# Gate units 0 to 7 as pairs on 64-row halves of TensorE in a fused linear-attention and gated-MLP kernel

## The chip, the cores and the metric

The kernel runs on one core of a Trainium2 chip. The metric is the device time of one execution in microseconds (us). TensorE (PE) does the matrix products and has its own stream of weight loads (PEld), VectorE (DVE) and ScalarE (ACT) take results out of PSUM and do the elementwise work, GpSimd (POOL) makes a few constants, SyncE (SP) issues most of the transfers. PSUM has 8 banks.

## The reference

The input `x` is 2048 tokens of 448 features, in bf16. Two branches start from the same layer norm and are multiplied:

```python
xn = _layernorm(x)
# branch s: 16 heads of 28, phi(t) = where(t > 0, t + 1, exp(t)) + 1e-6
q, k, v = split(xn @ wqkv)
kv  = einsum("bhsd,bhse->bhde", phi(k), v)
z   = einsum("bhsd->bhd", phi(k))
num = einsum("bhqd,bhde->bhqe", phi(q), kv)
den = einsum("bhqd,bhd->bhq", phi(q), z)[..., None] + 1e-6
s = (num / den).reshape(B, S, D) @ wo
# branch g: 448 -> 1792 -> 448
h = relu(xn @ w1 + b1) ** 2
g = silu(h @ w2 + b2)
out = x + s * g
```

## The kernel before

The tokens are cut into 16 tiles of 128, and those into 4 groups of 512. The work of TensorE is a sequence of units, written out in strings by hand at the end of the kernel function:

- `H{g}.{f}` (line 773): the hidden layer's 128 features `f` for the 512 tokens of group `g`. Its result is taken out by a relu with bias, on ACT (line 751) or DVE (line 748), and squared two units at a time, on DVE (line 762) or ACT (line 763), into `r2`.
- `K{t}` (line 716) and `Q{g}.{m}` (line 726): the keys of token tile `t`, and 128 columns of the queries of group `g`. `phi` takes each out by an exponential on ACT (line 694) and two operations on DVE (lines 699 and 706).
- `G{t}`, a gate unit: the product of token tile `t` of `r2` with `w_2`, 14 steps over 1792 features, 448 columns wide. DVE takes it out by adding `b2` (line 1069).
- `S{t}` (line 1171): the last product of the attention branch for a token tile.
- `P{t}` and `X{t}`: layer norm of four token tiles on DVE and ACT (lines 483 to 530), and their transpose into `xT` (two DVE operations, line 550, and 16 DMAs of 32 KB). Units of the group that begins with tile `t` read the result.
- `zs` (line 910): sums of phi(k) over the tokens on DVE. `R0 R1`, `Z`, `D` (lines 853, 924, 948) make the denominators, whose reciprocals go through DRAM and come back spread over the partitions (lines 966 to 1014).

The weights of H, K and Q have 448 rows, which is 3.5 times 128. So these units run in pairs on 64-row halves of the array: `pair` (line 654) runs, in one slot, one matmul of unit `a` on rows 0 to 63 and one of unit `c` on rows 64 to 127, in different PSUM banks. In a first phase `a` has the lower rows and `c` the upper ones, in a second phase they change places, and the first matmul of the second phase waits for the last of the first (`op.sync`). `pe_four` (line 685) lets two pairs alternate, first phases and then second phases, so that the work of the other pair lies between. The units G10 to G13 and all S run in such pairs too, through `weave` (line 1316), which steps each pair named by a word `A|B` each time the word comes up. A pair of gate units has 14 slots in a phase and is stepped four times, 7 slots each time.

The units G0 to G9 go through `gg` (line 1088, matmuls on line 1096) in another form: 14 matmuls on all 128 rows, in two parts of 7. In the strings they stand between pairs on 64 rows: G0 to G3 in one block, and G4, G5, G6 and G7 each alone.

The order on PE and SP is the program's order. For ACT, DVE and POOL, and for the PSUM banks, a planner (`Program.one_pass`, line 98) sorts the operations by modelled durations and due times before the kernel is built. Its model charges `SWITCH` for a change between 128-row and 64-row form, and an operation that empties a PSUM bank is due `BANK_LATE` after the start of the last matmul step that writes the bank. Each engine then executes its own list strictly in order, and waits on semaphores.

Of the kernel before, what the change touches and what calls it, by code (L numbers as in the profile page):

```python
# [18 lines left out]

LAT = {"pe": 0.2, "act": 0.07, "dve": 0.07, "pool": 0.08, "sp": 0.07}  # L20
SWITCH = 0.095
BANK_LATE = 6.5
SWAP = 1
PASSES = 1

# [21 lines left out]
class Program:  # L47
# [50 lines left out]
    def one_pass(self):  # L98
        ops = self.ops
        for op in reversed(ops):  # L100
# [3 lines left out]
            for r in op.reads:  # L104
                if isinstance(r, Buf):
                    late = min(late, self.writer[r].ideal + BANK_LATE)
            span = 14.0 if op.group else 4.5 if op.nbytes else op.dur + LAT[op.home]
# [198 lines left out]
def bass_recurrent_scan__linear_attn_block__dense_activation_squared_relu__prompt_kernel(  # L306
    nc, A_x, A_wqkv, A_wo, B_x, B_w1, B_b1, B_w2, B_b2, out
):
    with ExitStack() as es:
# [226 lines left out]
        def dve_transpose(lo):  # L536
            first = lo == 4 * SWAP
            parts = stage[:, :, :, :, :]
            stays = [("stage", 0), ("stage", 1)]
            if not first:  # L540
                parts = gbuf[:, NT - 5 : NT, :].rearrange("p t f -> p (t f)")[:, 0:2048]
                parts = parts.rearrange("p (b c j k) -> p b c j k", b=4, c=4, j=2)
                stays += [("g", i) for i in range(NT - 5, NT)]
            wide = parts.rearrange("p b c j k -> p (b c j k)").bitcast(f32)
            wide = wide.rearrange("p (b c j k) -> p c b j k", b=4, c=4, j=2)
            for j in range(2):
                src = xn[:, lo + 2 * j : lo + 2 * j + 2, :].rearrange("p t f -> p (t f)").bitcast(f32)
                src = src.rearrange("p (c b i) -> p c b i", c=4, b=4)
                add(
                    "dve", lambda e, _, j=j, src=src: e.transpose(wide[:, :, :, j, :], src),  # L550
                    [(n, lo + 2 * j + t) for n in ("xn", "xd") for t in (0, 1)], [stays[j]] + (stays[2:] if j else []), 0.7, label=f"tr{lo + 2 * j}",
                ).lead = 0.8 * (1 - j)
            for a in range(4):
                for b in range(4):
                    src = parts[32 * a : 32 * a + 32, b, :, :, :].rearrange("p c j k -> p (c j) k")
                    dst = by_group(slice(32 * b, 32 * b + 32), lo // 4).rearrange("p (n k) -> p n k", k=256)
                    by_act = lo == 4 and 4 * a + b > 12
                    op = dma(
                        "act" if by_act else "sp", dst[:, :, 64 * a : 64 * a + 64], src, [("xs", lo, a, b)], 32 * 1024,
                        stays, dur=0.65, slow=1.0,  # L560
                    )
                    op.group, op.lead = ("xs", lo), -8.0 if by_act else 0.0
# [65 lines left out]
        def pe_transpose_two(lo):  # L628
            b = Buf("T")

            def f(e, _):
                v = ps(b)[:, :].bitcast(bf)
                for i in range(8):
                    last = e.transpose(
                        v[:, i * P : (i + 1) * P], xn[:, lo + i // 4, (i % 4) * P : (i % 4 + 1) * P], ident[:, :]
                    )
                return last

            ts = (lo, lo + 1)
            add("pe", f, [(w, i) for i in ts for w in ("xn", "xd")] + ["ident"], [b], 8 * 0.065, mode="128", label=f"T{lo}")  # L640

            def ev(e, eng):
                src = ps(b)[:, :].bitcast(bf)
                dst = xT[:, lo : lo + 2, :, :].rearrange("p t c k -> p (t c k)")
                if eng == "dve":
                    return e.tensor_copy(dst, src)
                return e.activation(out=dst, in_=src, func=AF.Copy)

            add("dve", ev, [b], [("xT", i) for i in ts], 0.68, alts=[("act", 1.05)], label=f"eT{lo}")
# [35 lines left out]
        def pe_four(a, b, c, d):  # L685
            one, two = pair(a, c), pair(b, d)
            for p in (one, two, one, two):
                next(p)
            assert next(one, None) is next(two, None) is None
# [398 lines left out]
        def gg(si):  # L1088
            b = Buf("G")
            g = si // 4  # L1090
            for part in range(2):

                def f(e, _, part=part):
                    last = None
                    for fi in range(7 * part, 7 * part + 7):
                        last = e.matmul(  # L1096
                            ps(b)[:, 0:D], r_cols(slice(0, P), fi, si), w_2[:, fi, :], start=(fi == 0),
                            stop=(fi == NF - 1),
                        )
                    return last  # L1100

                add(
                    "pe", f, [("r2", g, fi) for fi in range(7 * part, 7 * part + 7)] + ["w2"] + ([b] if part else []), [b],
                    7 * MM(D), mode="128", label=f"G{si}.{part}",
                )
                if part:
                    g_bias(si, b)
                yield

        def silu(si):  # L1110
            if not silu_set:
                add(
                    "act", lambda e, _: e.preload_act_table_set("silu_and_others"), ["rden", "actw"], ["actw"], 1.3,
                    label="table2",
                )
                silu_set.append(1)
            gs = gbuf[:, si, :]
            add(
                "act", lambda e, _: e.activation(out=gs, in_=gs, func=AF.Silu), [("g", si), "actw"], [("g", si)], 0.577,  # L1119
                label=f"si{si}",  # L1120
            )
# [133 lines left out]
        def prep(lo):  # L1255
            ln(lo, lo + 2)
            ln(lo + 2, lo + 4)
# [15 lines left out]
        def run(text):  # L1273
            stream = []
            for w in text.split():
                assert not stream or w[0] in "KQHS", w
                if w[0] in "KQHS":
                    stream.append(w)
                    if len(stream) == 4:
                        pe_four(*map(unit, stream))  # L1280
                        stream.clear()
                elif w[0] == "G":
                    for _part in gg(int(w[1:])):
                        pass
                elif w[0] == "g":
                    next(sums.setdefault(w, gg(int(w[1:]))))
                elif w[0] == "X":
                    dve_transpose(int(w[1:]))
                elif w[0] == "T":
                    pe_transpose_two(int(w[1:]))  # L1290
                elif w[0] == "P":
                    prep(int(w[1:]))
                elif w[0] == "A":
                    for _part in token_sum(int(w[1:])):
                        pass
                elif w[0] == "a":
                    next(sums.setdefault(w, token_sum(int(w[1:]))))
                elif w[0] == "R":
                    q_rest(int(w[1:]))
                elif w == "zs":  # L1300
                    zsums()
                elif w == "Z":
                    z_cols()
                elif w == "D":
                    den()
                    spread()
                elif w == "V":
                    fold_wv()
                elif w == "M":
                    fold_wo()  # L1310
                elif w[0] == "I":
                    for v in w[1:].split(","):
                        silu(int(v))
            assert not stream

        def weave(text):
            pairs = {}
            for w in text.split():
                if w not in pairs:
                    pairs[w] = pair(*map(unit, w.split("|")))  # L1320
                next(pairs[w])
            assert all(next(p, 0) == 0 for p in pairs.values())

        hs = lambda g, lo, hi: " ".join(f"H{g}.{i + j}" for i in range(lo, hi, 4) for j in (0, 2, 1, 3)[: hi - i])
        gate = lambda a, b, u, v, more="": weave(
            f"G{a}|G{b} G{a}|G{b} {u}|{v} {more} G{a}|G{b} G{a}|G{b} {u}|{v} {more}"
        )
        run(hs(0, 2, 14) + " Q0.0 K2 Q0.1 K3 g0 g1 P8 g0 g1 G2 G3")
        run("X8 P12 " + hs(1, 0, 12) + " H1.12 K4 H1.13 K5 Q0.2 K6 Q1.0 K7 X12 G4 H2.0 Q1.1 H2.1 Q1.2 G5")
        run(hs(2, 2, 14) + " K8 Q2.0 K9 Q2.1 G6 H3.0 K10 H3.1 K11 H3.2 Q2.2 H3.3 Q3.0 G7 H3.4 K12 H3.5 K13")  # L1330
        run("H3.6 K14 H3.7 K15 zs H3.8 Q3.1 H3.9 Q3.2 H3.10 H3.11 H3.12 H3.13")
        run("R0 R1 a0 Z a0 D I0,1,2,3,4,5,6,7 a0 a0 A1 A2 A3 G8 V G9 M")
        a, b = "G10|G11", "G12|G13"
# [37 lines left out]
```

## Time and profile before

| | us |
|---|---|
| median of 3 runs (lowest, highest) | 146.09 (145.98, 146.63) |
| profiled execution | 146.12 |
| its span, first to last instruction | 144.0 |
| PE busy | 140.0 (97%) |
| DVE busy | 103.8 (72%) |
| ACT busy | 77.4 (54%) |
| weight loads | 71.4 (50%) |

Times in the text are microseconds from the start of the span. A line of the chain of work that ended last gives the start, the length, the engine, what is written, the line of the kernel and the number of instructions. A line of the timeline gives the start, the length from the first start to the last end, and the engine's instructions with their shapes. Starts of matmuls are recorded and their ends are modelled, so the distance from one start to the next is the safer number. In the table of windows each engine's busy time is followed by the number of instructions that started there.

### The profile page before, as it was taken

Reading aid. Unit: us, or ns where it says so; the run is one execution under the profiler, and the core shown is the slowest. Engines: PE = TensorE matmul, PEld = TensorE weight load, DVE = VectorE, ACT = ScalarE, POOL = GpSimd, SP = SyncE. Lnnn points to the kernel's source line nnn. Section 1 sums busy time; section 2 is a strip of 40 time slices with the busy share of each in tenths; the row PEclk is TensorE's granted clock in tenths of the full one; section 3 lists DMA queues with packets and bytes.
Section 4 is the critical chain, followed back from the end, with each engine's and each line's share of the span. In section 5 each row is a group of like instructions: output and inputs, shape, how many; then the busy total and the mean of one; then the engine's idle time right before and its main releaser. Section 6 shows DMA issues by size and latency. Waiting matters only on the chain.

```text
span 144.0 us, 3040 instructions
## 1 busy us (share of the span) xinstructions
PE 140.0 (97%) x1198; PEld 71.4 (50%) x1198; DVE 103.8 (72%) x225; ACT 77.4 (54%) x143; POOL 6.4 (4%) x40
## 2 busy tenths in 40 slices
PE   7999999999999999999999999999999999999991
PEld 7964444554444444444444444445547455555471
DVE  2779898699598799859778888971007736865874
ACT  3566977022588709597878378788239430302311
POOL 7900100000000000000000000000000000000000
PEclk9999999999999999999999999999999999999998
DMA  4999983496232100233000000000199400222032
GB/s 106 313 327 311 331 266 62 68 261 168 45 48 42 17 0 5 36 52 48 14 0 0 0 0 5 0 0 22 16 225 192 81 5 29 97 70 96 32 122 69
DMA packets 23499, 12.89 MB, mean 90 GB/s; under 512 B 14274, under 2 KB 22718, under 8 KB 23486
## 3 DMA queue, kind: packets, MB, share of 16 engines
q1 hardware_dynamic: 21758, 11.40, 30.7%
q10 hardware_dynamic: 1728, 1.31, 4.1%
q8 instruction: 9, 0.15, 0.4%
q14 instruction: 4, 0.03, 0.1%
HBM read 9.23 MB, written 1.90 MB: 77 GB/s over the span
## 4 chain that ended last, share of the span: by engine, by line
PE 96%; DVE 2%; issue 0%
PE pb L773 29%; PE pb L1096 19%; PE pb L1079 7%; PE pb L1171 7%; PE pb L874 6%; PE pb L716 6%; PE pb L726 6%; PE pb L1206 4%; PE pb L1136 3%; PE pb L853 1%; DVE gbuf L1160 1%; PE pb L880 1%; PE pb L816 1%; PE pb L788 1%; PE pb L1023 1%; PE pb L948 1%
## 5 line engine op out<-in xcount | busy, mean ns | idle before, releaser
L773 PE MATMUL pb<-xT,w 64*128 64x512 bf16 x378 | 43.6, 376 | 0.0
L751 ACT ACTIVATE r<-pb,b1f 128x512 bf16<-128x512 f32 x39 | 25.3, 686 | 19.0 <-PE pb L773 18.2
L773 PEld LDWEIGHTS pb<-xT,w 64*128 64x128 bf16 x378 | 18.0, 94 | 22.6 <-issue 1.1
L1096 PE MATMUL pb<-w,r 128*128 128x448 bf16 x140 | 27.7, 353 | 0.0
L1096 PEld LDWEIGHTS pb<-w,r 128*128 128x128 bf16 x140 | 13.2, 98 | 13.9 <-issue 1.2
L748 DVE TENSOR_SCALAR r<-pb,b1f 128x512 bf16<-128x512 f32 x17 | 12.4, 745 | 5.4 <-PE pb L773 5.4
L763 ACT ACTIVATE r<-r 128x1024 bf16<-128x1024 bf16 x15 | 15.7, 1062 | 0.4 <-DVE r L748 0.3
L1191 DVE TENSOR_TENSOR gbuf<-pb,gbuf 128x448 bf16<-128x448 f32 x14 | 8.1, 618 | 6.1 <-PE pb L1171 6.1
L1079 PE MATMUL pb<-w,r 64*128 64x448 bf16 x112 | 11.7, 349 | 0.0
L716 PE MATMUL pb<-w_k,xT 64*128 64x448 bf16 x98 | 11.6, 349 | 0.0
L987 DVE TENSOR_TENSOR pqT<-pqT,xT 128x2048 bf16<-128x2048 bf16 x3 | 3.7, 1218 | 10.7 <-DMA xT<-scr 10.7
L1069 DVE TENSOR_TENSOR gbuf<-pb,b2b 128x448 bf16<-128x448 f32 x14 | 8.5, 617 | 3.6 <-PE pb L1096 2.1
L726 PE MATMUL pb<-xT,w_q 64*128 64x512 bf16 x84 | 11.0, 376 | 0.0
L483 DVE BATCH_NORM_STATS2 st<-x_tok 128x6 f32<-128x448 bf16 x16 | 9.3, 611 | 2.4 <-DMA x_tok<-in_A_x_dram 2.4
L1119 ACT ACTIVATE gbuf<-gbuf 128x448 bf16<-128x448 bf16 x14 | 7.0, 570 | 6.8 <-DVE gbuf L1069 5.9
L1171 PE MATMUL pb<-w_k,pqT 64*128 64x448 bf16 x96 | 10.5, 349 | 0.0
L874 PE MATMUL pb<-pk,xn 128*128 128x448 bf16 x48 | 9.6, 353 | 0.0
L706 DVE SCALAR_TENSOR_TENSOR pk<-pb,pk 128x448 bf16<-128x448 f32 x16 | 9.3, 617 | 0.1
L762 DVE TENSOR_TENSOR r<-r 128x1024 bf16<-128x1024 bf16 x13 | 8.4, 685 | 0.2
L694 ACT ACTIVATE pk<-pb 128x448 bf16<-128x448 f32 x16 | 7.8, 545 | 1.3 <-PE pb L803 0.7
L910 DVE TENSOR_TENSOR zacc<-zacc,pk 128x448 f32<-128x448 f32 x13 | 8.0, 619 | 0.2
L1079 PEld LDWEIGHTS pb<-w,r 64*128 64x128 bf16 x112 | 5.4, 94 | 5.3 <-issue 0.4
(98 smaller groups left out, 141.3 us busy)
## 6 DMA issues: line engine op xcount, KB each, us to landing
out_dram<-gbuf SPq DMA_DIRECT2D x15, 112.0 KB, 1.7
w<-in_B_w_dram SPq DMA_DIRECT2D x1, 1568.0 KB, 9.5
x_tok<-in_A_x_dram SPq DMA_DIRECT2D x3, 448.0 KB, 5.7
xT<-gbuf SPq DMA_DIRECT2D x32, 32.0 KB, 2.0
w<-in_B_w_dram SPq DMA_DIRECT2D x2, 384.0 KB, 5.8
xT<-scr SPq DMA_DIRECT2D x6, 112.0 KB
w<-in_B_w_dram SPq DMA_DIRECT2D x1, 576.0 KB, 5.6
xT<-scr ACTq DMA_DIRECT2D x5, 112.0 KB
```

The lines of the kernel that those rows point to most:

```text
L483: add("dve", lambda e, _: e.bn_stats(st6[:, si, :], x_tok[:, si, :]), [("x", si)], [("st", si)], 0.61, label=f"bn{si}").prio = hp(si, 0)
L706: lambda e, _: e.scalar_tensor_tensor(out=slot, in0=ps(buf)[0:rows, 0:n], scalar=1.0 + 1e-6, in1=slot, op0=ALU.add, op1=ALU.max),
L716: return e.matmul(ps(b)[:, 0:D], x_tile(rows, si, c), w_k[rows, c, :], start=start, stop=stop)
L726: return e.matmul(ps(b)[:, 0:512], w_q[rows, c, m * P : (m + 1) * P], x_group(rows, g, c), start=start, stop=stop,)
L748: return e.tensor_scalar(out=slot, in0=ps(b)[:, 0:512], scalar1=b1f[:, fi : fi + 1], scalar2=0.0, op0=ALU.add, op1=ALU.max)
L751: return e.activation(out=slot, in_=ps(b)[:, 0:512], func=AF.Relu, bias=b1f[:, fi : fi + 1])
L763: return e.activation(out=both, in_=both, func=AF.Square)
L773: return e.matmul(ps(b)[:, 0:512], w_1[rows, c, fi * P : (fi + 1) * P], x_group(rows, g, c), start=start, stop=stop,)
L874: last = e.matmul(ps(b)[:, 0:D], xn_cols(si, c * P, (c + 1) * P), pk[:, si, :], start=(si == 0), stop=(si == NT - 1),)
L1079: return e.matmul(ps(b)[:, 0:D], r_cols(rows, fi, si), w_2[rows, fi, :], start=start, stop=stop)
L1096: last = e.matmul(ps(b)[:, 0:D], r_cols(slice(0, P), fi, si), w_2[:, fi, :], start=(fi == 0), stop=(fi == NF - 1),)
L1171: return e.matmul(ps(b)[:, 0:D], w, msb[rows, c, :], start=start, stop=stop)
```

## The change

G0 to G7 leave `gg` and go through `pair` on 64-row halves. G0|G1 alternates with G2|G3. G4|G5 is interleaved with the pairs H2.0|H2.1 and Q1.1|Q1.2, which before made a `pe_four` between G4 and G5. G6|G7 is interleaved with H3.0|H3.1 and K10|K11, which before made a `pe_four` between G6 and G7; the units H3.2, Q2.2, H3.3 and Q3.0 now come behind G7 and not ahead of it. `weave` passes a word without `|` on to `run`, so that P8 keeps a place inside the block of G0 to G3. `BANK_LATE` goes from 6.5 to 8.0, which changes due times of all PSUM operations in the planner. G8 and later units and the end of the kernel are as before.

```diff
-BANK_LATE = 6.5
+BANK_LATE = 8.0
@@ weave
             for w in text.split():
+                if "|" not in w:
+                    run(w)
+                    continue
                 if w not in pairs:
                     pairs[w] = pair(*map(unit, w.split("|")))
                 next(pairs[w])
@@ the order of the units
-        run(hs(0, 2, 14) + " Q0.0 K2 Q0.1 K3 g0 g1 P8 g0 g1 G2 G3")
-        run("X8 P12 " + hs(1, 0, 12) + " H1.12 K4 H1.13 K5 Q0.2 K6 Q1.0 K7 X12 G4 H2.0 Q1.1 H2.1 Q1.2 G5")
-        run(hs(2, 2, 14) + " K8 Q2.0 K9 Q2.1 G6 H3.0 K10 H3.1 K11 H3.2 Q2.2 H3.3 Q3.0 G7 H3.4 K12 H3.5 K13")
+        run(hs(0, 2, 14) + " Q0.0 K2 Q0.1 K3")
+        weave("G0|G1 G0|G1 G2|G3 P8 G2|G3 G0|G1 G0|G1 G2|G3 G2|G3")
+        run("X8 P12 " + hs(1, 0, 12) + " H1.12 K4 H1.13 K5 Q0.2 K6 Q1.0 K7 X12")
+        weave("G4|G5 G4|G5 H2.0|H2.1 G4|G5 H2.0|H2.1 Q1.1|Q1.2 G4|G5 Q1.1|Q1.2")
+        run(hs(2, 2, 14) + " K8 Q2.0 K9 Q2.1")
+        weave("G6|G7 G6|G7 H3.0|H3.1 G6|G7 H3.0|H3.1 K10|K11 G6|G7 K10|K11")
+        run("H3.2 Q2.2 H3.3 Q3.0 H3.4 K12 H3.5 K13")
         run("H3.6 K14 H3.7 K15 zs H3.8 Q3.1 H3.9 Q3.2 H3.10 H3.11 H3.12 H3.13")
```

`hs(g, lo, hi)` lists the units H of group `g` from `lo` to `hi` in the order in which `pe_four` pairs neighbours.

## The prediction

> **What bounds the kernel now.** I read the first page, then the chain that ended last, then the waits of PE, then the timeline around the gates.
>
> ```profile
> PE 140.0 (97%) x1198; PEld 71.4 (50%) x1198; DVE 103.8 (72%) x225; ACT 77.4 (54%) x143; POOL 6.4 (4%) x40
> PEclk9999999999999999999999999999999999999998
> PE 96%; DVE 2%; issue 0%
> ```
>
> PE is busy from end to end at the full granted clock, and 96% of the chain is PE. The waits of PE hold one entry, at the start:
>
> ```profile
> PE pb L1206 <- DVE dum L368: 1.1, 1, 1.1
> ```
>
> So nothing that the other engines do holds PE up. Only what PE itself does counts, as long as the others keep up. In the chain, by start and length:
>
> ```profile
> 22.79 0.57 PE pb L716 x6
> 23.35 10.70 PE pb L1096 x56
> 34.05 10.03 PE pb L773 x92
> ...
> 57.53 9.17 PE pb L773 x84
> 66.70 0.76 PE pb L716 x8
> ...
> 114.28 2.75 PE pb L1079 x28
> 117.03 0.76 PE pb L1171 x8
> 117.79 1.32 PE pb L1079 x14
> ```
>
> L1096 is a gate on 128 rows, L1079 a gate pair on 64-row halves (G10 to G13). The last line is 7 slots of two matmuls in 1.32, or 0.189 a slot. The timeline gives recorded starts around G4:
>
> ```profile
> 47.51 0.81 PE L726 MATMUL pb<-xT,w_q 64*128 64x512 bf16 x6
> 48.16 0.73 PE L716 MATMUL pb<-w_k,xT 64*128 64x448 bf16 x6
> 48.83 2.82 PE L1096 MATMUL pb<-w,r 128*128 128x448 bf16 x14
> 51.58 1.04 PE L773 MATMUL pb<-xT,w 64*128 64x512 bf16 x8
> ```
>
> K takes 3 slots, 0.567, yet G4 starts 0.67 behind it: 0.10 is lost on entering the 128-row form. G4's 14 matmuls at 0.189 are 2.65, yet H starts 2.75 behind G4: 0.10 on leaving. No wait is named there.
>
> **The change part by part.**
>
> *The matmuls themselves: zero.* 8 gates x 14 = 112 matmuls of 128 rows become 224 on halves, two to a slot, again 112 slots. G0 to G3 take 10.70 - 0.10 = 10.60 for 56 matmuls, 0.1893 each; the slot of L1079 is 1.32 / 7 = 0.1886. The difference, 112 x 0.0007 = 0.08, is within rounding. I take 0 and keep a gain of 0.1 for the range.
>
> *The weight loads: zero.* A half load takes 94 ns (row L773 PEld; L1079 likewise), a whole one 98, and now there are two in a slot. In the G10|G11 stretch of the table of windows:
>
> ```profile
> 24.00:33.00 9.00, 9.00 (x50) 4.66 (x48) 7.70 (x20) 1.96 (x7) 0.00 (x0) 1.00 0.67 155
> 114.50:117.00 2.50, 2.50 (x30) 1.27 (x28) 1.82 (x3) 2.05 (x5) 0.00 (x0) 1.00 0.00 0
> ```
>
> 28 half loads occupy PEld for 1.27, not 28 x 0.094 = 2.63: the two of a slot overlap. If they did not, 2 x 97 ns (the longest) = 194 ns would exceed the slot by 5 ns, 0.55 over 112 slots; that is the upper bound. The Trainium skill (TensorE: Matmul & The Clock Gate, section LDWEIGHTS) speaks against the change here: it gives P/1.2 ns for a load of P columns whatever the number of rows. An estimate from it for two loads one behind the other is 213 ns a slot and 2.7 us in all; the trace agrees that half the rows save nothing (94 against 98 ns), but shows less per load and the overlap, so the measurement decides.
>
> *The form switches: about -1.05.* Before there are five blocks in 128-row form among 64-row work: G0 to G3, G4, G5, G6, G7, so ten switches. From starts, the five entries (22.62 to 23.29, 48.16 to 48.83, 53.96 to 54.71, 68.72 to 69.47, 77.44 to 78.19, less 3 slots of 0.189 or 0.216) lose 0.10 each and the exits 0.10 to 0.11. Ten are 1.0 to 1.1. After the change K, G and H are all on halves, and where L1079 and L1171 alternate, 14 instructions take 1.32 throughout, so a change of unit alone costs nothing. G8 and later units keep their switches.
>
> *The added waits on PE: zero.* Each second phase waits for the last matmul of its first phase, and everything on PE queues behind. The smallest distance is one step of H or Q, 8 instructions or 0.86 (between G4|G5's phases, and G6|G7's). K8|K9's second phase stands 0.86 behind its first today (66.54 + 0.76 to 68.16) without a gap. Bounds: 0, and 4 pairs x 0.35 (one matmul's length) = 1.4 if none were covered. I take 0, the same form being shown.
>
> *Inputs earlier.* G0|G1 needs features 7 to 13 of `r2` 1.32 behind its start, at about 24.5; before, G0's second part came 2.65 behind it. DVE's six squares end at 23.06 before. In the new order one relu (0.7) stands among them, not ahead, and ACT takes the other: still about 23.2. Cover 1.3. P8's first statistics now stand ahead of the phi of Q0, waiting for `x_tok`: issued at 12.07, landed 10.5 later, 22.6, in time.
>
> *Evictions in twos and later.* The new DVE order puts all four L1069 of G0 to G3 behind P8 and both transposes of X8. Adding row means from 23.2 (statistics 1.2, phi of Q0 and K2, K3 delayed by ACT's three DMA issues that now stand ahead of their exponentials, to 27.7, norm and transposes to 32.9), they run 32.9 to 35.3; before, the last ended at 35.86. The banks of G0 to G3 are wanted by the second `pe_four` of H1 at 36.8. Cover 1.5. The later `BANK_LATE` costs nothing else while such covers hold. G4|G5 ends at 56.4, its evictions at about 58.2, wanted at 60.0. G6|G7 ends at 76.5, evictions 77.8, wanted at 80.1.
>
> *The transfers.* X8's 16 DMAs on SP start some 2 earlier; H2 wants them at 51.3. X12's follow its transposes, 57.45 before:
>
> ```profile
> 56.16 1.29 DVE L550 STREAM_TRANSPOSE gbuf<-xn 128x512 f32<-128x512 f32 x2
> ```
>
> The last issue ended at 67.88 and landing takes 2.0, so 69.9, 12.45 behind the transposes. H3.0 moves from 72.3 to 71.5. I walk the transposes' end to 56.7 (DVE is then no more loaded, and G4's eviction no longer stands between). Cover 2.3.
>
> *The closing stretch.* From 77.0 to R0 at 91.8 no gate gives DVE time to catch up. DVE's list there, by row means: K phi 3 x 1.6, Q phi 2 x 1.8, relus 1.5, sums and `zb` 4.0, about 13.9 in 14.8 and some waits for exponentials. Walked through with PE's new times it reaches the phi of R0 at 92.6, and R0's exponential ends at 93.5: cover 0.9. The tightest banks are K14|K15's (Q2.2's phi ends 82.9, wanted 83.8) and H3.12|H3.13's (88.9 for 89.6). None runs out. Before, the same point:
>
> ```profile
> 93.09 0.21 DVE L910 TENSOR_TENSOR zb<-zacc,pk 128x64 bf16<-128x64 f32 x1
> 94.48 0.29 DVE L699 TENSOR_SCALAR pqR<-pqR 128x512 bf16<-128x512 bf16 x1 [1.18 <-ACT pqR L694]
> ```
>
> DVE waited there 1.18 for ACT, which followed PE, so the reciprocals, their DMAs and S0 all shift with PE. The tail is unchanged.
>
> **Sum.** -1.05 and nothing given back: span 144.0 to 142.95. The profiled execution took 146.12, 2.12 of it around the span, and lies 0.03 above the median of 146.09. 146.12 - 1.05 = 145.07, say 145.1, 0.7% less than 146.09. A measurement of this kernel tells about 0.5%, 0.73, from no change.
>
> **The rivals.**
>
> *DVE falls behind in the closing stretch (slower).* D is in order on PE, and A cannot pass it. DVE has 0.9 to spare at R0's phi and 0.35 more at D (`zsb` ended at 96.01, D started at 96.36). Each us of lateness beyond 1.25 costs PE one; from 2.3 the gain is gone, and from 3.0 the kernel is slower by over 0.5%. For it: DVE was busy 16.75 of the 20 us from 77 to 97, and the gates G6 and G7, 2.75 each, no longer lie in it as pauses. Against it: the sums (9.2 in all) are begun early, and G7's stretch had idle time of DVE for lack of data. At a lateness of 3.3: 145.1 + 2.05 = 147.1.
>
> *Small stalls at banks.* The covers of 0.7 to 0.9 come from a walk that adds means. If two or three are missed by 0.2 to 0.4 each, 0.4 to 1.0 comes back: 145.5 to 146.1. The planner's order is fixed by modelled times and not by these rows.
>
> *The switch does not go.* If the 0.10 belongs to a gate's first wait and not to the form, it stays: 146.1. Against it: leaving a gate costs as much, the 56 matmuls of G0 to G3 start three gates without it, and so does each pair at L1171.
>
> *The loads bind.* With loads one behind another at 194 ns: +0.55, 145.6. The overlap shown speaks against it. By the page's figure named above it would be 147.8.
>
> **How the numbers follow.** Forecast 0.67; small stalls 0.14; switch stays 0.03; loads bind 0.03; DVE behind 0.13. The last alone is slower: 0.13. The three before it are within 0.5%: 0.20. Faster: 0.67. The forecast's own range is 144.9 to 145.4 (1.1 and 0.1 off, or 0.3 back). For 8 in 10 I add the small stalls, the loads and the mild end of DVE's lateness (2.5 late, 146.4), and below 0.2 for the slot and the switches: 144.8 to 146.4.
>
> **What would show it.** Right: L1079 x112 in the chain at 10.6 between K and H, 14 instructions per 1.32, no switch of 0.10 at any of the ten places, R0 at about 91.8, D at 95.4, and PE's waits still with one entry. Wrong: a wait of PE for DVE or ACT near 36.8, 60, 71.5, 83.8, 89.6 or 95.4, or a slot of L1079 above 0.19.

## The result, and the profile after

The changed kernel takes 144.70 us (median; 144.64 to 144.81) where the kernel before, run beside it, takes 146.22 (145.98 to 146.63): a ratio of 0.989, 95% interval 0.986 to 0.993. A second, longer comparison (below) gives 144.84 against 146.12, ratio 0.991 (0.989 to 0.992). The forecast was 145.1, so the direction and the mechanism came out, and the time is lower than forecast, by 0.4 and 0.3. Both medians lie below the forecast's own range of 144.9 to 145.4; of the wider range of 144.8 to 146.4 the first lies 0.1 below and the second just inside.

The profiled execution took 144.75, with a span of 143.0. The forecast of the span was 142.95. What lies around the span went from 2.12 to 1.75, where the forecast had left it alone.

The page of the changed kernel, the lines that answer to those shown of before:

```profile
PE 139.0 (97%) x1310; PEld 72.2 (50%) x1310; DVE 104.3 (73%) x226; ACT 77.2 (54%) x142; POOL 6.4 (4%) x40
PEclk9999999999999999999999999999999999999999
PE 96%; DVE 2%; issue 0%
```

PE still runs from end to end at the full granted clock. Its waits have the same single entry as before, at the start:

```profile
PE pb L1206 <- DVE dum L368: 1.1, 1, 1.1
```

So no wait came in the place of what was removed. In the chain (start, length, engine and line, instructions) the gates now run as 64-row pairs, L1079, between the same neighbours:

```profile
11.51 9.06 PE pb L773 x84
...
22.84 0.57 PE pb L716 x6
23.41 10.59 PE pb L1079 x112
34.00 9.93 PE pb L773 x92
...
48.17 0.57 PE pb L716 x6
48.74 2.65 PE pb L1079 x28
51.38 0.86 PE pb L773 x8
52.25 1.32 PE pb L1079 x14
53.57 0.65 PE pb L773 x6
...
57.05 9.06 PE pb L773 x84
...
91.82 1.85 PE pb L853 x16
...
95.41 0.98 PE pb L948 x16
...
140.78 0.26 DVE gbuf L1160
```

Compare pairs of lines with before. G0 to G3 were 10.70 and the H units behind them 10.03; now they are 10.59 and 9.93, 0.11 and 0.10 less with the same number of slots. The 84 H instructions behind G5 were 9.17 and are 9.06. The interleaved gates take 1.32 per 14 instructions, seven slots of 0.189, and the steps of H between them 0.86 and 0.65, four and three slots of 0.216. R0 and D start at 91.82 and 95.41; forecast were 91.8 and 95.4.

The timeline of PE (start, length from first start to last end) shows the same in recorded starts, at the place where 0.10 was lost twice before:

```profile
48.01 0.73 PE L716 MATMUL pb<-w_k,xT 64*128 64x448 bf16 x6
48.57 2.81 PE L1079 MATMUL pb<-w,r 64*128 64x448 bf16 x28
51.22 1.03 PE L773 MATMUL pb<-xT,w 64*128 64x512 bf16 x8
```

K's three slots are 0.57, and G4|G5 starts 0.56 behind K. Its 14 slots are 2.65, and H starts 2.65 behind it. Nothing is lost on either side.

The head of the kernel, up to the first of the 84 H instructions of the first block, varies from execution to execution with the landing of the first loads. To take it out, the text below compares the rest: the span less the start of `L773 x84` in the chain. This is 144.0 - 11.45 = 132.55 before and 143.0 - 11.51 = 131.49 after: 1.06 less, where 1.05 was forecast. From here on this rest is what stands "behind the head". The same lines of the chain before:

```profile
11.45 9.06 PE pb L773 x84
...
141.78 0.26 DVE gbuf L1160
```

The span is given to 0.1 only. From the first of the 84 H to the chain's last piece, DVE's last operation, both starts are given to 0.01: 141.78 - 11.45 = 130.33 before and 140.78 - 11.51 = 129.27 after, again 1.06 less.

### The profile page after: what moved, and what is told of

Read it like the earlier page. It is cut to its first block, busy times and chain, and to the rows that moved or that the text cites. A ratio compares the mean times of both kernels' runs of the same rounds, so it can differ in the third digit from the quotient of the medians.

```text
span 143.0 us, 3268 instructions
## 1 busy us (share of the span) xinstructions
PE 139.0 (97%) x1310; PEld 72.2 (50%) x1310; DVE 104.3 (73%) x226; ACT 77.2 (54%) x142; POOL 6.4 (4%) x40
## 4 chain that ended last, share of the span: by engine, by line
PE 96%; DVE 2%; issue 0%
PE pb L773 29%; PE pb L1079 22%; PE pb L1171 7%; PE pb L874 7%; PE pb L716 6%; PE pb L726 6%; PE pb L1206 4%; PE pb L1096 4%; PE pb L1136 3%; PE pb L853 1%; DVE gbuf L1160 1%; PE pb L880 1%; PE pb L816 1%; PE pb L1023 1%; PE pb L788 1%; PE pb L590 1%
## 5 line engine op out<-in xcount | busy, mean ns | idle before, releaser
L773 PE MATMUL pb<-xT,w 64*128 64x512 bf16 x378 | 43.6, 376 | 0.0
L1079 PE MATMUL pb<-w,r 64*128 64x448 bf16 x336 | 34.1, 349 | 0.0
L751 ACT ACTIVATE r<-pb,b1f 128x512 bf16<-128x512 f32 x40 | 25.9, 687 | 14.2 <-PE pb L773 13.4
L773 PEld LDWEIGHTS pb<-xT,w 64*128 64x128 bf16 x378 | 18.4, 94 | 21.7
L1079 PEld LDWEIGHTS pb<-w,r 64*128 64x128 bf16 x336 | 16.3, 94 | 15.8 <-issue 0.4
L748 DVE TENSOR_SCALAR r<-pb,b1f 128x512 bf16<-128x512 f32 x16 | 11.7, 748 | 5.5 <-PE pb L773 5.3
L763 ACT ACTIVATE r<-r 128x1024 bf16<-128x1024 bf16 x14 | 14.6, 1061 | 0.5 <-DVE r L748 0.4
L762 DVE TENSOR_TENSOR r<-r 128x1024 bf16<-128x1024 bf16 x14 | 9.1, 683 | 0.1
L694 ACT ACTIVATE pqT<-pb 128x512 bf16<-128x512 f32 x12 | 6.5, 597 | 3.3 <-PE pb L726 3.3
L706 DVE SCALAR_TENSOR_TENSOR pqT<-pb,pqT 128x512 bf16<-128x512 f32 x12 | 7.8, 683 | 0.1
```

What stands on the lines that cost most here:

```text
L694: "act", lambda e, _: e.activation(out=slot, in_=ps(buf)[0:rows, 0:n], func=AF.Exp), [buf, "actw"],
L706: lambda e, _: e.scalar_tensor_tensor(out=slot, in0=ps(buf)[0:rows, 0:n], scalar=1.0 + 1e-6, in1=slot, op0=ALU.add, op1=ALU.max),
L748: return e.tensor_scalar(out=slot, in0=ps(b)[:, 0:512], scalar1=b1f[:, fi : fi + 1], scalar2=0.0, op0=ALU.add, op1=ALU.max)
L751: return e.activation(out=slot, in_=ps(b)[:, 0:512], func=AF.Relu, bias=b1f[:, fi : fi + 1])
L763: return e.activation(out=both, in_=both, func=AF.Square)
L773: return e.matmul(ps(b)[:, 0:512], w_1[rows, c, fi * P : (fi + 1) * P], x_group(rows, g, c), start=start, stop=stop,)
```

## The experiments

Twelve runs follow, the first of them of the changed kernel itself. "Outside" is the time of an execution less its span. The number in brackets behind a median counts the executions. A diff is against the kernel that the text names; in diffs, `...` marks lines left out.

**The changed kernel again, longer.** No edit. The question was whether the fall of what lies outside the span belongs to the kernel or to one execution.

> The changed kernel once more, beside the kernel before on the same chip, to settle where 144.7 came from when the span (143.0) was as forecast. Theory A, the miss is the time around the span, which differs from one chip or execution to the next and not from one of the two kernels to the other: on one chip both have the same time outside the span, and the difference of the medians is that of the spans, 1.0 to 1.1 us (ratio 0.9925 to 0.993). Theory B, the change also shortens what lies outside the span: the changed kernel has about 1.75 us outside and the kernel before about 2.1, and the medians differ by 1.4 to 1.6 us (ratio 0.989 to 0.9905). In both the span is 142.9 to 143.1.

Measured: 144.84 (6) against 146.12 (21), ratio 0.991 (0.989 to 0.992). Outside was 1.68 to 1.77, mean 1.73, over six executions, and 2.00 to 2.12, mean 2.05, over the 21 of the kernel before: the two do not overlap. The mean spans are 143.13 and 144.11. So of the 1.3 us between the kernels 1.0 is span and 0.3 lies outside it, and the 0.3 belongs to the kernel. It had to be explained apart from the span. The repeat also shows how far two traces of one kernel agree: behind the head the profiled execution is 143.5 - 11.97 = 131.53, for 131.49 in the first, and from the first H to DVE's last operation it is 129.27 in both.

**G0 to G3 alone as pairs.** Only the block of G0 to G3 is changed, which takes away two form switches; G4 to G7 stay as before. The diff is against the changed kernel, and `BANK_LATE` stays at 8.0.

```diff
-        run("X8 P12 " + hs(1, 0, 12) + " H1.12 K4 H1.13 K5 Q0.2 K6 Q1.0 K7 X12")
-        weave("G4|G5 G4|G5 H2.0|H2.1 G4|G5 H2.0|H2.1 Q1.1|Q1.2 G4|G5 Q1.1|Q1.2")
-        run(hs(2, 2, 14) + " K8 Q2.0 K9 Q2.1")
-        weave("G6|G7 G6|G7 H3.0|H3.1 G6|G7 H3.0|H3.1 K10|K11 G6|G7 K10|K11")
-        run("H3.2 Q2.2 H3.3 Q3.0 H3.4 K12 H3.5 K13")
+        run("X8 P12 " + hs(1, 0, 12) + " H1.12 K4 H1.13 K5 Q0.2 K6 Q1.0 K7 X12 G4 H2.0 Q1.1 H2.1 Q1.2 G5")
+        run(hs(2, 2, 14) + " K8 Q2.0 K9 Q2.1 G6 H3.0 K10 H3.1 K11 H3.2 Q2.2 H3.3 Q3.0 G7 H3.4 K12 H3.5 K13")
```

> Only G0 to G3 as pairs on halves; G4 to G7 stay in 128-row form; the due time of evictions is 8.0 as in the changed kernel. Two of ten form switches go. Theory of the form switch (0.10 to 0.106 each): 0.21 us below before, span 143.8, ratio about 0.9985. Rival, the gain comes from how the evictions and the layer norm lie around the block of four gates, so that most of it is here: 0.7 us or more below before.

Measured: 146.03 (12), ratio 1.000 (0.999 to 1.002). Behind the head the profiled execution is 143.9 - 11.55 = 132.35, 0.20 less than before, as the theory of the switches has it; outside is 2.06, as before. A gain of 0.2 is below what the medians can tell here. Its chain shows where the loss is gone and where it is not:

```profile
23.45 10.59 PE pb L1079 x112
34.04 9.93 PE pb L773 x92
...
48.77 2.76 PE pb L1096 x14
51.53 0.97 PE pb L773 x8
```

G0 to G3 have the changed kernel's 10.59 and 9.93; G4, still on 128 rows, keeps 2.76, and the H behind it 0.97 in place of 0.86.

**G4 to G7 alone as pairs.** The other part of the change, eight switches. Again the diff is against the changed kernel.

```diff
-        run(hs(0, 2, 14) + " Q0.0 K2 Q0.1 K3")
-        weave("G0|G1 G0|G1 G2|G3 P8 G2|G3 G0|G1 G0|G1 G2|G3 G2|G3")
+        run(hs(0, 2, 14) + " Q0.0 K2 Q0.1 K3 g0 g1 P8 g0 g1 G2 G3")
```

> Only G4 to G7 as pairs, interleaved with two H and two Q or two K as in the changed kernel; G0 to G3 stay in 128-row form in one block. Eight of ten switches go. Theory of the form switch: 0.84 us below before, span 143.15, ratio about 0.994. Rival, gain of the block of four gates: 0.3 us or less below before.

Measured: 144.96 (6), ratio 0.993 (0.991 to 0.994). Behind the head 143.7 - 11.84 = 131.86. Of this 0.18 stands ahead of all gates: the first 84 H instructions took 9.24 in this execution, 9.06 in the others. The timeline of PEld has a wait there, for a relu of ACT:

```profile
12.67 7.91 PEld L773 LDWEIGHTS pb<-xT,w 64*128 64x128 bf16 x76 [0.46 <-ACT r L751]
```

Without the 0.18 it is 131.68, 0.87 less than before, or 0.109 for each of eight switches. Outside is 1.74: the fall outside the span came with this part.

**The new order with the gates on 128 rows.** The interleaving stays, every gate unit goes through `gg` in two parts where the changed kernel steps the pair. This makes 14 switches in place of ten. The diff is against the changed kernel.

```diff
-        weave("G0|G1 G0|G1 G2|G3 P8 G2|G3 G0|G1 G0|G1 G2|G3 G2|G3")
+        run("g0 g1 P8 g0 g1 G2 G3")
...
-        weave("G4|G5 G4|G5 H2.0|H2.1 G4|G5 H2.0|H2.1 Q1.1|Q1.2 G4|G5 Q1.1|Q1.2")
+        weave("g4 g5 H2.0|H2.1 g4 H2.0|H2.1 Q1.1|Q1.2 g5 Q1.1|Q1.2")
...
-        weave("G6|G7 G6|G7 H3.0|H3.1 G6|G7 H3.0|H3.1 K10|K11 G6|G7 K10|K11")
+        weave("g6 g7 H3.0|H3.1 g6 H3.0|H3.1 K10|K11 g7 K10|K11")
```

> The changed kernel's order of units, its interleaving with H, Q and K and its due times, but gates 0 to 7 in 128-row form, stepped in halves of 7 matmuls: G0 to G3 one block as before; G4 and G5, then G4, then G5, and the same with G6 and G7, so seven blocks in 128-row form instead of five and fourteen switches. Theory of the form switch: 14 x 0.105 = 1.5 us above the changed kernel and 0.4 above before: span 144.4 to 144.5, ratio to before 1.003. Rival, the order of the work is what gained (evictions in twos, transposes earlier): as fast as the changed kernel, or between it and before: span 143.0 to 143.9.

Measured: 146.51 (10), ratio 1.002 (1.001 to 1.003), slower, as expected. Behind the head 144.4 - 11.42 = 132.98, 0.43 more than before for four more switches. Outside is 2.04. Its chain:

```profile
48.86 2.75 PE pb L1096 x14
51.61 0.97 PE pb L773 x8
52.58 1.43 PE pb L1096 x7
54.01 0.76 PE pb L773 x6
```

Each piece that follows a change of form is 0.10 to 0.11 longer than the same piece in the changed kernel: 2.75 for 2.65, 0.97 for 0.86, 1.43 for 1.32, 0.76 for 0.65. The order of the units by itself brings nothing; the form does.

**`BANK_LATE` alone.** The kernel before with the planner's figure of the changed one.

```diff
-BANK_LATE = 6.5
+BANK_LATE = 8.0
```

> The kernel before with BANK_LATE 8.0 and nothing else: PE's order is the same, evictions and layer norm stand in another order on DVE and ACT; ACT's list stays at 185. Theory, this part of the change only moves work within cover: span from the first H of the 84 to the end unchanged (132.55 before), 2.05 outside, ratio 1.000. Rival, later evictions make PE wait for banks, or earlier transposes gain: 0.3 or more off either way.

Measured: 146.29 (10), ratio 1.001 (0.999 to 1.003). Behind the head 144.1 - 11.52 = 132.58 against 132.55; outside 2.05. It does nothing here, neither in the span nor beside it.

**What the fall outside the span goes with.** The kernels so far fall in two groups, 1.73 to 1.74 and 2.04 to 2.06, with nothing between. Between the groups, the engines' instruction lists in the built programs differ in length (waits that stand as instructions of their own are counted). ACT's list has 185 instructions in the kernel before, in G0 to G3 alone, in the new order on 128 rows and with `BANK_LATE` alone, and 183 in the changed kernel and in G4 to G7 alone: the planner's new order for ACT needs one operation less and one separate wait less. DVE's list is 252 or 253 where the time outside is 2.04 to 2.06, and 254 where it is 1.73 to 1.74; PE's is at most 1297 (G0 to G3 alone) in the former and at least 1302 (G4 to G7 alone) in the latter. Four kernels try the lists one by one.

First, the changed kernel with ACT's list back at 185, by two copies of 16 columns into a spare tile, which compute nothing that is used:

```diff
...
+                    def copy(e, _):
+                        for k in range(2 if si == 14 else 0):
+                            e.activation(out=spare[:, k, :], in_=ps(b)[:, 0:16], func=AF.Copy)
+                        return e.activation(out=xn[:, si, 0:D], in_=ps(b)[:, 0:D], func=AF.Copy)
...
```

> The changed kernel with two tiny extra operations on ACT (16 columns each, into a spare tile, ahead of the copy of S14), which make its list as long as that of the kernel before (185 instructions instead of 183). The time outside the span was 2.04 to 2.06 for the kernels with 185 on ACT (before, block_only, order_128) and 1.73 to 1.74 for those with 183 (changed, four_only), with a spread of 0.04. Theory, it goes with the length of ACT's list: 2.05 outside the span here. Rivals, it goes with the lists of DVE (254 or more is short) or PE (1302 or more is short): 1.73 here. The span is 143.0 to 143.5 in any case.

Measured: 145.13 (1), span 143.1, outside 2.03. The lists of DVE (254) and PE are those of the changed kernel here, so neither of them sets the time outside. Behind the head it is 143.1 - 11.57 = 131.53, as in the repeat of the changed kernel.

Second, the kernel before with two DVE operations of 16 columns ahead of `zb`, which makes DVE's list 254, that of the changed kernel:

```diff
...
+                        for k in range(2 if i == NT - 1 and n == D else 0):
+                            e.tensor_tensor(out=spare[:, k, :], in0=prev[:, 0:16], in1=pk[:, i, 0:16], op=ALU.add)
...
```

> The kernel before with two tiny extra operations on DVE (16 columns each, into a spare tile, ahead of zb), so 254 instructions instead of 252. Theory, the time outside the span goes with DVE's list: 1.73. Rivals, ACT's or PE's: 2.05. The span is 144.0 to 144.4 in any case.

Measured: 146.05 (1), span 144.0, outside 2.05.

Third, the kernel before with 64 more matmuls of 32 columns behind the last gate, on zeros, into a bank that nothing reads:

```diff
...
+        def more(e, _):
+            for _i in range(64):
+                last = e.matmul(ps(tail)[0:32, 0:32], dum[:, 0:32], dum[:, 0:32], start=True, stop=True)
+            return last
+
+        add("pe", more, ["dum"], [tail], 64 * 0.03, mode="12832", label="more")
```

> The kernel before with 64 tiny matmuls (32 columns of zeros) behind the last gate, beside the closing work of DVE and the last transfers, so 1306 instructions on PE instead of 1242. Theory, the time outside the span goes with PE's list: 1.73. Rivals, ACT's or DVE's: 2.05. The span is 144.0 to 144.4 in any case.

Measured: 148.24 (1), span 146.2, outside 2.04. PE's list has 1306 instructions here, more than in G4 to G7 alone (1302, 1.74), and the time outside is that of the kernel before: PE's list is not it. The expectation of the span was missed. It was to stay near 144 and grew by 2.2, of which 0.22 is a later head (the first of the 84 H starts at 11.67, 11.45 before). The kernel's own steps kept their places behind it: DVE's last operation ends at 142.3, 142.0 before. But the last two output transfers land late. The DMA queues and issues in the stretch from 142 to 143 of this kernel (packets, MB, share of 16 engines; KB each, us from issue to landing):

```profile
q1 hardware_dynamic: 135, 0.11, 33.6%
q10 hardware_dynamic: 133, 0.06, 20.7%
q8 instruction: 1, 0.02, 10.7%
issues: line engine op xcount, KB each, median us to landing
out_dram<-gbuf ACTq DMA_DIRECT2D x1, 64.0 KB, 3.7
out_dram<-gbuf SPq DMA_DIRECT2D x1, 48.0 KB, 3.4
```

In the kernel before these two take 1.6 and 1.5 to land. A transfer of instructions (0.02 MB in one packet, 10.7% of 16 engines for 1 us, so 1.7 us on one engine) starts among them, which the kernel before does not have behind 130; no packet moves from 143.6 to 144, and 27 packets of the two output queues follow from 144 to 145.3. The delay of 2 lies there. That the instruction packet held up the output packets behind it on its DMA engine fits these rows; it was not tried by itself.

Fourth, the kernel before with ACT's list shortened to 181: the last transfers of reciprocals, issued by SP and ACT in turn, are all issued by SP. Three issues move (the expectation says two), so SP's list grows from 116 to 119, and the planner gives one copy of ACT's to DVE.

```diff
-                        ("sp", "act")[n % 2], dst, ap(r, [[0, q - p], [1024, 2], [1, 512]]),
+                        "sp", dst, ap(r, [[0, q - p], [1024, 2], [1, 512]]),
```

> The kernel before, with the two DMAs on ACT's queue among the last four that bring the reciprocals back moved to SP's; the planner then also gives one copy of M to DVE and not to ACT, so ACT's list is 181 instructions and not 185, SP's 119 and not 116. Theory, the time outside the span goes with the length of ACT's list and falls by 0.31 between 185 and 183: 1.74 outside the span, the span as before (144.0 to 144.2), median about 145.8, ratio 0.998. Rival, it fell in the changed kernel through something that the pairs do and rose in act_plus2 through the two operations' place near the end: 2.05 here, ratio 1.000.

Measured: 145.99 (10) against 146.12 (23), ratio 0.998 (0.996 to 1.000). Outside was 1.68 to 1.78, mean 1.72, over ten executions, against 1.99 to 2.09, mean 2.04, over the 23 beside it. The gates are on 128 rows, the order is that of before, and the 0.3 is gone all the same. The span did not shrink (means 144.31 and 144.22); 0.1 of it went the other way, which hides part of the gain in the median.

So the 0.3 outside goes with ACT's list, from both sides: lengthened by two in the changed kernel it comes back, shortened by four in the kernel before it goes. The two edits touch different operations and have the length of ACT's list in common. The 64-row form as such does not set it.

**How much room DVE had in the closing stretch.** The rival that ended slower was DVE late at D. This kernel is the changed one with 16 more DVE operations on 64 columns ahead of `zb`.

```diff
...
+                        for k in range(16 if i == NT - 1 and n == D else 0):
+                            e.tensor_tensor(out=spare[:, k, :], in0=prev[:, 0:64], in1=pk[:, i, 0:64], op=ALU.add)
...
```

> The changed kernel with 16 extra operations of 64 columns on DVE ahead of zb, into a spare tile, some 2.2 to 3.2 us (0.14 to 0.2 each), with everything else in the same order. It tests how far DVE is from bounding the closing stretch. In the changed kernel DVE waits 1.38 for ACT ahead of the phi of R0, and zsb ends 0.34 ahead of D, so about 1.7 is to spare by the profile and 1.25 by the forecast's walk. Theory: PE waits at Z or D for the extra time less 1.7 (0.5 to 1.5), and the span grows by as much. Rival that DVE already bounds the stretch: the span grows by the whole extra time. Rival that there is more cover than the profile shows: no wait, span 142.9 to 143.5.

Measured: 144.93 (1), span 143.2, outside 1.73. Behind the head 143.2 - 11.37 = 131.83, 0.34 more than the changed kernel. The timeline of DVE and that of PE in this kernel, the added work and the wait that it causes:

```profile
89.59 2.26 DVE L911 TENSOR_TENSOR spare<-zacc,pk 128x64 bf16<-128x64 f32 x16
```

```profile
95.53 0.83 PE L951 MATMUL pb<-pqT,zsb 128*32 128x512 bf16 x12 [0.26 <-DVE zsb L934]
```

About 2.2 us of added DVE work cost PE 0.26 to 0.34. The room was therefore about 1.9. Without the added work, the timeline of DVE in the changed kernel:

```profile
93.48 0.29 DVE L699 TENSOR_SCALAR pqR<-pqR 128x512 bf16<-128x512 bf16 x1 [1.38 <-ACT pqR L694]
...
94.67 0.33 DVE L931 TENSOR_TENSOR zsb<-pb,zmask 128x160 bf16<-128x160 f32 x1
```

DVE stands idle for 1.38 ahead of the phi of R0 (forecast 0.9), and `zsb` ends at 95.0, 0.35 ahead of D: 1.7 by the rows, 1.25 by the forecast's walk.

**A form switch that is left, moved away.** A0 to A3 (lines 874 and 880) are sums over the tokens of products of phi(k) and the normalised tokens; `a0` is a step of A0. A3 has the form 128*64 in the timeline, the other three and G8 have 128*128. In the closing stretch A3 runs ahead of G8. Moved to stand right behind R0 R1, it lets G8 follow work from which G8 loses nothing. Two versions of the changed kernel:

```diff
-        run("R0 R1 a0 Z a0 D I0,1,2,3,4,5,6,7 a0 a0 A1 A2 A3 G8 V G9 M")
+        run("R0 R1 A3 a0 Z a0 D I0,1,2,3,4,5,6,7 a0 a0 A1 A2 G8 V G9 M")
```

> The changed kernel with the token sum A3 (128 rows, 64 columns) moved from behind A2 to behind R1, which has the same form. That takes away two more form switches, A2 to A3 and A3 to G8. Theory of the form switch: 0.2 us below the changed kernel, span 142.75 to 142.85. Rival: the denominators D, the reciprocals, their transfers and the products with the queries come 1.64 us later, the last of which ended 0.55 ahead of S0 in the changed kernel, so that PE waits up to 1.1 at S0: span 143.0 to 144.0.

Measured: 144.88 (4), ratio 0.991 (0.988 to 0.994). Behind the head 143.0 - 11.20 = 131.80, 0.3 more than the changed kernel. A wait came in place of the switch. The waits of PE and, for its cause, the timeline of DVE:

```profile
PE pb L1171 <- DVE pqR L1009: 0.3, 1, 0.3
```

```profile
115.06 0.69 DVE L1009 TENSOR_TENSOR pqR<-pqR,xT 128x1024 bf16<-128x1024 bf16 x1 [0.26 <-DMA xT<-scr]
```

D stood 1.5 later behind the head, so the reciprocals came back later, DVE waited 0.26 for the last of them, and S0 waited for DVE. By recorded starts S0 begins 3.14 behind the gate pair ahead of it, 2.66 in the changed kernel: 0.48 is lost there, more than the 0.2 that two switches bring.

The second version takes one step `a0` (0.78) from ahead of D to behind it, so that A3 (1.51) delays D by 0.76 and not by 1.5:

```diff
-        run("R0 R1 a0 Z a0 D I0,1,2,3,4,5,6,7 a0 a0 A1 A2 A3 G8 V G9 M")
+        run("R0 R1 A3 Z a0 D I0,1,2,3,4,5,6,7 a0 a0 a0 A1 A2 G8 V G9 M")
```

> The changed kernel with A3 behind R1, and Z directly behind A3 and one part of A0 less ahead of D, so that D comes 0.8 later than in the changed kernel and not 1.64 as in a3_early, where PE waited 0.3 at S0 for the last transfer of the reciprocals. Two form switches fewer (A2 to A3, A3 to G8). Theory of the form switch: from the first H of the 84 to the end 131.3 and not 131.5, no wait at S0, median 0.2 below the changed kernel, ratio to before 0.9895. Rival, the transfers are still late: a wait at S0, 131.5 or more.

Measured: 144.80 (6), ratio 0.989 (0.986 to 0.991). Behind the head 142.6 - 11.27 = 131.33, 0.16 less than the changed kernel, and no wait at S0. Its chain has G8 without the loss:

```profile
96.91 8.43 PE pb L874 x44
105.34 2.65 PE pb L1096 x14
```

In the changed kernel the same G8 takes 2.76. This version is the shortest behind the head of all that ran, but its median can't be told from the changed kernel's 144.70 and 144.84.

## Why the prediction was right, and where it was not

**The form switches (-1.05): right, and shown.** The profiled executions give these differences against before, behind the head and, given more finely, from the first of the 84 H to DVE's last operation (both times less the 0.18 in G4 to G7 alone):

| kernel | switches at G0 to G7 | behind the head, us | per switch | to DVE's last, us | per switch |
|---|---|---|---|---|---|
| new order on 128 rows | 14 | +0.43 | 0.108 | +0.43 | 0.108 |
| before | 10 | 0 | | 0 | |
| G0 to G3 alone | 8 | -0.20 | 0.100 | -0.22 | 0.110 |
| G4 to G7 alone | 2 | -0.87 | 0.109 | -0.86 | 0.108 |
| changed kernel | 0 | -1.06 | 0.106 | -1.06 | 0.106 |

One price fits all five kernels, and `BANK_LATE` alone gives 0.00 by the finer measure. The rival "the switch does not go" falls. The Trainium skill (TensorEngine Tiling (Array Packing), section Key Properties) says that a change of the tiling mode drains TensorE. The runs agree that such a change costs time, 0.10 to 0.11 us each; that it is a drain, they do not show.

**Matmuls and weight loads (zero): right.** The 56 slots of L1079 (112 instructions) take 10.59 in the block of G0 to G3, 0.189 each, and 1.32 per 7 slots elsewhere. For the loads, the table of windows of the changed kernel, the block and the G10|G11 stretch (stretch; total, then busy time and count of PE, PEld, DVE, ACT, POOL; clock, DMA share, GB/s):

```profile
23.50:33.50 10.00, 10.00 (x110) 5.13 (x108) 9.61 (x25) 2.65 (x8) 0.00 (x0) 1.00 0.51 122
114.00:116.50 2.50, 2.50 (x30) 1.31 (x28) 1.31 (x2) 1.55 (x4) 0.00 (x0) 1.00 0.00 0
```

108 half loads of 94 ns would be 10.2 one behind another; they occupy PEld for 5.13, so the two of a slot overlap here too, and the rival "the loads bind" falls. The Trainium skill's figure (TensorE: Matmul & The Clock Gate, section LDWEIGHTS) of P/1.2 ns a load, by which the forecast estimated 2.7 us more for loads one behind the other, does not show here; the measurement decides.

**The added waits on PE, the inputs earlier, the transfers, the evictions (zero each): right.** PE has no wait behind the start. The walks of the forecast stand against rows of the changed kernel's DVE timeline: the squares were to end at 23.2 and end at 23.18; X12's transposes were to end at 56.7 and end at 56.47; the evictions of G4|G5 were to end at 58.2 and end at 57.6. The evictions of G0 to G3 were walked to 32.9 to 35.3:

```profile
32.68 1.11 DVE L1069 TENSOR_TENSOR gbuf<-pb,b2b 128x448 bf16<-128x448 f32 x2
34.04 1.16 DVE L1069 TENSOR_TENSOR gbuf<-pb,b2b 128x448 bf16<-128x448 f32 x2 [0.25 <-PE pb L1079]
```

They end at 35.2, and the forecast has the banks wanted at 36.8. One step of the walk was off: `x_tok` was to be there at 22.6, and DVE waited 0.61 for it, until 23.78. It cost nothing, because the covers behind it (the time to spare before PE would have to wait) held. So the rival "small stalls at banks" did not come.

**The closing stretch (zero): right.** The cover was underestimated, 1.25 against 1.7 by the rows and about 1.9 by the experiment. The rival "DVE behind" needed DVE to be late by 1.75 beyond its cover to end slower; none of the cover was used up.

**The step that failed: "2.12 of it around the span".** The sum took the gain off the span, where it was right (-1.06 behind the head for -1.05), and kept the 2.12 around the span as it was, without a reason. It fell by 0.31 to 0.33 (means of many executions; 0.37 between the two profiled ones). With -0.31 the forecast's own sum is 144.76, between the two medians measured. There was a hint: the planner sorts ACT's list anew, so the change could touch ACT's instructions and not only PE's. It could not be priced from one kernel's trace. The range's lower bound was made of terms of the span alone (0.2 below for slot and switches), so it had no room for this term.

**What stays open.** Why the length of ACT's list sets the time outside the span, whether that time lies ahead of the first recorded instruction or behind the last, and whether the step lies at 184 or 185 instructions: none of it was tried. The Trainium skill (Runtime: NRT & Kernel Launch, section Instruction fetch mechanics) says that instructions are fetched in blocks of 256. The recorded transfers of instructions inside the span do not sort the two groups: queue q8 has 9 packets in the kernel before (2.05) and with ACT's list at 181 (1.72), 10 in G0 to G3 alone (2.06) and in the changed kernel (1.73), and q14 has 4 in all of them.

## What to carry to other kernels

Where PE is busy from end to end, look for losses between its own instructions: the distance of recorded starts, less the slots between them, priced a change of matmul form at 0.10 to 0.11 us here, and counting changes gave the gain. A cover found by adding row means held everywhere here, but a move that delays a long round trip (D to S0, 1.5 us too late in one experiment) turns the gain into a wait. Look at the time outside the span as a term of its own, in every execution: it can step with something as remote as another engine's list.

## What was not expected of the hardware

- The time outside the span takes two values, 1.72 to 1.75 and 2.03 to 2.06 (means, or the one execution of a kernel), and nothing between. With 181 to 183 instructions in ACT's list it is the lower, with 185 the higher, in kernels of both forms.
- 64 small matmuls at the end (1.8 us on PE, beside the last evictions) lengthened the span by 2.2, although no result waited for them: a transfer of instructions came among the last output transfers, which landed 2 us later.
- Between traces of one kernel, most of the spread lies ahead of the first block: the two of the changed kernel have spans of 143.0 and 143.5, the block starts at 11.51 and 11.97, and behind it they agree to 0.04. Where a head was long, its PE waited for `w_k` (0.8 in the repeat of the changed kernel) or for the layer norm of `x_tok` (0.9 in G4 to G7 alone). The executions of the kernel before have spans from 143.8 to 144.9; only one of them was traced, so there the place of the spread is not shown.
